# A tuned attention kernel: one of four head pairs goes from TensorE transposes to DMA transposes, with a new order

## The chip, the cores and the metric

The kernel runs on one core of a Trainium2 chip. The core has five engines with a queue each: TensorE (PE; its weight loads are shown as PEld), VectorE (DVE), ScalarE (ACT), GpSimd (POOL) and SyncE (SP), which here only issues transfers. The metric is the device time of one execution in microseconds (us); the median of three executions before the change is 809.87 us (809.32 to 811.25).

## The reference

Two attention layers follow each other. The first has 8 batches, 8 heads, 576 positions and 64 numbers a head. A score stays in the softmax only if it is within tau of its row's largest:

```python
scores = scale * np.matmul(q, k.transpose(0, 1, 3, 2))
thresh = np.max(scores, axis=-1, keepdims=True) - tau
scores = np.where(scores >= thresh, scores, -1000000000.0)
attn = softmax(scores)
x = concat_heads(attn @ v)              # 8 x 576 x 512
```

The second is a causal attention with four experts of one head each. Two of four experts are chosen for a position by gate logits, and their outputs are added with their weights:

```python
logits = x @ w_gate                     # the two largest of four, softmax over them: w
for e in range(4):
    a = softmax(causal(scale * (x @ wq[e]) @ (x @ wk[e]).T))
    out += w[..., e] * (a @ (x @ wv[e]) @ wo[e])
```

## The kernel before, in words

The 64 heads are worked on as 32 pairs, n = 0 to 31, four pairs a batch (n % 4 is 0 to 3). Both heads of a pair lie beside each other on the 128 partitions. The 576 queries of a head make four tiles of 128 and a rest of 64; the rests of two neighbouring pairs share one more tile, which comes with the odd pair. So an even pair has four query tiles and an odd pair five.

For each pair `prep` loads keys, queries and values (`ki`, `qi`, `vz`) and transposes keys and queries on PE into `kx` and `qx`. For each query tile, `scores` does this: PE multiplies (`kx`, `qx`) into PSUM, two banks a head (family "s"). DVE copies the scores to `pp` and takes the row's extreme (line 750). ACT applies the threshold (line 768) and the exponential with its sum (line 762). Then the paths part, by `on_pe(n)`:

- On PE: POOL scales `pp`. `transp` transposes it on PE in blocks (16 half transposes a tile, line 1306), DVE copies the blocks to `pa` (line 690), and ACT copies the rests to `pb`. `attnv32` multiplies with the values in fp32.
- By DMA: POOL writes the rounded half of `hl` in fp16 (line 716), and DVE the residual (line 739). `turned` issues one DMA transpose for the whole tile on SP's queue (`hl` to `T`, line 1032), and `attnv` multiplies in fp16, three products for one (the halves of weights and values). The values are split into fp16 halves `vh` once a pair, by a scale that comes from their largest number (a DVE reduction, a small PE product with `ones`, line 890, POOL, DVE line 739).

Before, the first four pairs (`FIRST = 4`) and of the later batches the third and fourth pair (`TURNED = 2, 3`) go on PE; the first and second pair of the seven later batches go by DMA: 7 x (4 + 5) = 63 transposes.

When a batch's four pairs are done, `moe` does the second layer for it: projections (fp32, rounded parts), gates, causal scores, transposes on PE, values and output. It is laid among the pairs of the next batch; only the last batch's has nothing beside it.

The order is not that of the code. Each operation is recorded with a place: a pair number plus a number from the table `PLACE`, and one by engine and tile from `PLACE_OP`. `arrange` goes through time with estimated durations, picks the ready operation of lowest rank for each engine, gives out buffers and PSUM banks, and so fixes the order of each engine's queue. Each engine then works its queue strictly in order. `fill` puts small matmuls on `still` into PE's planned gaps of the first 160 us. Buffers: two `hl`, three `T`, one `ki`, one `qi`, two `vz`.

Of the kernel before, what the change touches and what calls it, by code (L numbers as in the profile page):

```python
# [30 lines left out]
FIRST = 4  # L31
TURNED = 2, 3
# [50 lines left out]
    "ovload": -58.26292, "ovx": 0.6755247, "ovy": 0.919954, "perm": 3.2453, "qT": -0.3301571, "qload": 0.1930829,  # L83
# [102 lines left out]
class Plan:  # L186
# [43 lines left out]
    def op(self, e, busy, late, outs, ins, fn):  # L230
        o = Op(e, busy, late, outs, ins, fn, self.place)
        n = len(self.ops)
# [334 lines left out]
def kernel(  # L567
# [297 lines left out]
    def unit(n, name):  # L865
        plan.place = (n, ("", "o", "c", "d")[n % NPAIR] + name)
# [470 lines left out]
```

## Time and profile before

| | |
|---|---|
| median of 3 runs | 809.87 us |
| profiled execution | 809.53 us |
| its span, first to last instruction | 807.8 us |
| granted TensorE clock, mean | 0.997 |
| PE busy | 788.8 us (98%) |
| PE weight loads busy | 661.3 us (82%) |
| DVE busy | 678.7 us (84%) |
| ACT busy | 680.9 us (84%) |
| POOL busy | 346.3 us (43%) |
| DMA transposes T<-hl | 63, median 4.8 us from issue to landing |

An engine's busy time counts the instructions it carries out, not those that only issue a transfer. A group of instructions is shown with its busy time, the mean time of one, and the idle time of the engine just before it with what ended it. The chain of waits follows the last instruction back to the start, at each step to what released it.

### The profile page before, as it was taken

Reading aid. Unit: us, or ns where it says so; the run is one execution under the profiler, and the core shown is the slowest. Engines: PE = TensorE matmul, PEld = TensorE weight load, DVE = VectorE, ACT = ScalarE, POOL = GpSimd, SP = SyncE. Lnnn points to the kernel's source line nnn. Section 1 sums busy time; section 2 is a strip of 40 time slices with the busy share of each in tenths; the row PEclk is TensorE's granted clock in tenths of the full one; section 3 lists DMA queues with packets and bytes.
Section 4 is the critical chain, followed back from the end, with each engine's and each line's share of the span. In section 5 each row is a group of like instructions: output and inputs, shape, how many; then the busy total and the mean of one; then the engine's idle time right before and its main releaser. Section 6 shows DMA issues by size and latency. Waiting matters only on the chain.

```text
span 807.8 us, 27956 instructions
## 1 busy us (share of the span) xinstructions
PE 788.8 (98%) x10986; PEld 661.3 (82%) x10986; DVE 678.7 (84%) x2147; ACT 680.9 (84%) x1834; POOL 346.3 (43%) x494
## 2 busy tenths in 40 slices
PE   8999999999999999999999999999999999999998
PEld 6777888788778888788888897878878788878986
DVE  3889889988998889988899788998799888998284
ACT  3889889987999879898799988999799987989373
POOL 5764326433454326532275323643246432564110
PEclk9999999999999999999999999999999999999999
DMA  8431567427591356714575165642647227660002
GB/s 164 103 71 46 119 107 123 93 56 144 109 166 36 90 108 153 139 41 114 104 154 107 43 134 114 145 97 57 145 99 139 50 68 132 129 118 16 15 14 93
DMA packets 253604, 79.87 MB, mean 99 GB/s; under 512 B 240288, under 2 KB 248736, under 8 KB 253472
## 3 DMA queue, kind: packets, MB, share of 16 engines
q1 hardware_dynamic: 251744, 77.69, 46.7%
q8 instruction: 86, 1.41, 0.7%
q10 hardware_dynamic: 1728, 0.39, 0.3%
q14 instruction: 46, 0.38, 0.1%
HBM read 31.47 MB, written 9.44 MB: 51 GB/s over the span
## 4 chain that ended last, share of the span: by engine, by line
PE 69%; DVE 15%; DMA 6%; ACT 5%; issue 2%; POOL 1%; SPq 0%; POOLq 0%; ACTq 0%; DVEq 0%
PE banks L653 60%; PE banks L1306 9%; DVE pp L750 5%; DMA T<-hl 4%; DVE hl L739 2%; ACT pp L768 2%; DVE p L745 2%; DVE pa L690 2%; ACT pp L762 2%; DVE col L716 1%; DVE col L715 1%; POOL hl L716 1%; DMA lg<-in_moe_w_gate_dram 1%; DMA qi<-in_q_dram 0%; ACT pt L688 0%
## 5 line engine op out<-in xcount | busy, mean ns | idle before, releaser
L768 ACT ACTIVATE pp<-pp,col 128x576 f32<-128x576 f32 x286 | 212.1, 776 | 31.7 <-DVE col L716 27.1
L750 DVE TENSOR_SCALAR_CACHE_REDUCE pp<-banks 128x576 f32<-128x576 f32 x286 | 207.9, 749 | 16.4 <-PE banks L653 13.9
L762 ACT ACTIVATE pp<-pp 128x576 f32<-128x576 f32 x286 | 195.1, 685 | 1.0
L716 POOL TENSOR_SCALAR pp<-pp,col 128x576 f32<-128x576 f32 x160 | 123.9, 785 | 136.3 <-DVE col L728 88.9
L653 PE MATMUL banks<-kx,qx 64*128 64x288 f32 x1024 | 157.5, 422 | 0.8 <-DVE pp L750 0.3
L716 POOL TENSOR_SCALAR hl<-pp,col 128x576 f16<-128x576 f32 x126 | 93.7, 756 | 114.5 <-DMA T<-hl 37.7
L739 DVE SCALAR_TENSOR_TENSOR hl<-pp,col,hl 128x576 f16<-128x576 f32 x126 | 117.3, 944 | 29.5 <-POOL hl L716 29.5
L716 POOL TENSOR_SCALAR p<-p,col,gw 128x256 f32<-128x256 f32 (+3 forms) x114 | 75.9, 676 | 131.5 <-PE banks L653 49.8
L653 PEld LDWEIGHTS banks<-kx,qx 64*128 64x128 f32 x1024 | 92.2, 187 | 24.8 <-issue 4.7
L690 DVE COPY pa<-banks 128x512 f32<-128x512 f32 x152 | 96.8, 681 | 4.6 <-PE banks L1306 4.5
L762 ACT ACTIVATE p<-p,col 128x384 f32<-128x384 f32 (+4 forms) x136 | 78.4, 580 | 24.9 <-DVE col L745 24.0
L653 PE MATMUL banks<-pa,vz 128*64 128x128 f32 (+1 forms) x1344 | 82.0, 266 | 0.3 <-DVE pt L690 0.2
L745 DVE CUSTOM_DVE_ANT_0 p<-banks,mask 128x384 f32<-128x384 f32 (+4 forms) x136 | 66.1, 504 | 13.8 <-PE banks L653 13.8
L653 PEld LDWEIGHTS banks<-pa,vz 128*64 128x64 f32 x1344 | 68.8, 137 | 7.2 <-issue 3.0
L1306 PEld LDWEIGHTS banks<-ident,pp 64*128 64x128 f32 x1492 | 57.5, 139 | 15.6 <-issue 5.1
L653 PE MATMUL banks<-wvh,x 128*128 128x260 f32 x320 | 66.1, 289 | 2.9 <-DVE col L745 2.9
L1306 PE MATMUL banks<-ident,pp 64*128 64x64 f32 x1492 | 66.3, 227 | 1.3 <-DVE pp L750 0.7
L653 PEld LDWEIGHTS <-vh 128*64 128x64 f16 x2100 | 54.6, 111 | 11.2 <-DMA T<-hl 5.8
L653 PE MATMUL banks<-T,vh 128*64 128x128 f16 (+1 forms) x2100 | 59.0, 215 | 4.0 <-DMA T<-hl 3.3
L653 PEld LDWEIGHTS banks<-wvh,x 128*128 128x128 f32 x320 | 52.1, 188 | 8.7 <-DVE col L745 5.9
L688 ACT ACTIVATE pt<-banks 128x384 f32<-128x384 f32 (+2 forms) x128 | 56.9, 503 | 0.9 <-PE banks L1306 0.8
L762 ACT ACTIVATION_READ_ACCUMULATOR pp<-pp 128x1 f32 x286 | 57.5, 201 | 0.0
(143 smaller groups left out, 1623.6 us busy)
## 6 DMA issues: line engine op xcount, KB each, us to landing
ki<-in_k_dram SPq DMA_DIRECT2D x32, 256.0 KB, 3.7
vz<-in_v_dram SPq DMA_DIRECT2D x32, 256.0 KB, 2.8
qi<-in_q_dram SPq DMA_DIRECT2D x62, 128.0 KB, 2.9
out_dram<-st SPq DMA_DIRECT2D x30, 256.0 KB, 2.6
tk<-in_k_dram SPq DMA_DIRECT2D x16, 128.0 KB, 3.9
vz<-in_v_dram SPq DMA_DIRECT2D x64, 16.0 KB, 2.4
out_dram<-st SPq DMA_DIRECT2D x8, 128.0 KB, 2.3
T<-hl SPq DMA_TRANSPOSE x63, 4.8
```

The source lines that it names most:

```text
L653: lambda o, x, y: nc.tensor.matmul(o, x, y, start=start, stop=stop))
L688: run(e, t, [dst], [src], lambda d, s: nc.scalar.activation(d, s, AF.Copy))
L690: run(e, t, [dst], [src], lambda d, s: nc.vector.tensor_copy(d, s))
L715: return m.tensor_scalar(d, s, x_, None, op0=op0)
L716: return m.tensor_scalar(d, s, x_, y_, op0=op0, op1=op1)
L739: return nc.vector.scalar_tensor_tensor(d, a_, x_, r.pop(0), op0=op0, op1=op1, **kw)
L745: lambda o, a, i, m: nc.vector.tensor_tensor_reduce(o, i, m, 1.0, 3e38, ALU.add, ALU.min, a))
L750: lambda o, a, i: nc.vector.tensor_scalar(o, i, 1.0, None, op0=ALU.mult, op1=ALU.min, accum_out=a))
L762: return nc.scalar.activation(d, s, AF.Exp, scale=scale, **kw)
L768: lambda d, s, x: nc.scalar.activation(d, s, AF.Prelu, bias=x, scale=-1.0, alpha=1e36))
L1306: o.fn(*(r.place() for r in (*o.outs, *o.ins)))
```

## The change

- `TURNED = (3,)`: the third pair of the seven later batches goes by DMA transposes. 28 tiles change path: 7 x (4 + 5 + 4) = 91 transposes. `on_pe` also has a new term with `FINAL = 0`, which changes nothing at that value. The third pair's values are now split into `vh`.
- A head's two banks of scores may be any two of the eight, not only neighbours.
- For the first pair the keys come first on SP's queue and the queries first on ACT's, with the first two heads of the tails; tau and the first weights come after. The other heads' tails are loaded later, in their own transfers.
- All places of the order are new (`PLACE`, `PLACE_OP`; a new name for the place of `hl`, and the planned issue time of some transfers), of which a line or two is shown.

```diff
-TURNED = 2, 3
+TURNED = (3,)
+FINAL = 0
...
-    "LMo0": 37.77021, "LMo1": 59.55178, "LMo2": 59.18834, "LMo3": 6.447113, "LMo4": 4, "La00": 81.09086,
+    "LMo0": 83.62052, "LMo1": 44.69387, "LMo2": 32.21728, "LMo3": 16.53009, "LMo4": 4, "La00": 83.36004,
...
+PSUMS = "s", "g"
...
-    plan.family("s", [Slot([("b", i), ("b", i + 1)], lambda *_, i=i: banks[:, i:i + 2]) for i in range(7)])
+    plan.family("s", [Slot([("b", i), ("b", i + d)], lambda *_, i=i, d=d: banks[:, i:i + d + 1:d])
+                      for d in range(1, 8) for i in range(8 - d)])
...
-        busy = 580 if e == "SP" and more == 0 else 650
+        busy = 580 if e == "SP" and more == 0 else 700
...
-    plan.place = (-36.0, "load")
+    plan.place = (-320.0, "load")
     dma(tau_t, bass.AP(tensor=tau.tensor, offset=tau.offset, ap=[[0, P], [1, 1]]), "ACT", 1)
...
-        plan.place = (n, ("", "o", "c", "d")[n % NPAIR] + name)
+        plan.place = (n, ("", "o", "c", "d")[n % (2 if n >= NPR - FINAL else NPAIR)] + name)
 
     def on_pe(n):
-        return n < FIRST or n % NPAIR in TURNED
+        return n < FIRST or n % NPAIR in TURNED and n < NPR - FINAL
...
         if not n:
-            plan.place = (-30.0, "load")
+            plan.place = (-430.0, "load")
         dma(ki, ks, "SP", more)
         unit(n, "qload")
         if not n:
-            plan.place = (-29.0, "load")
+            plan.place = (-530.0, "load")
         for j in range(2):
             dma(qi[:, :, j], qs[:, :, j], eq, more)
         if n == 0 or n % NPAIR == 1 and b < B - 1:
-            plan.place = (n, "tload") if n else (-22.0, "load")
             c = b + (n > 0)
             tk, tq = (tails.setdefault((c, x), plan.tile(x, [P, H, D], F32)) for x in ("tk", "tq"))
-            for rows in heads:
-                dma(tk[rows], k[c, :, SM:, :].rearrange("h p d -> p h d"), "SP", more)
-            dma(tq[heads[0]], q[c, :, SM:, :].rearrange("h p d -> p h d"), eq, more)
+            for part in (slice(0, 2), slice(2, H)) if n == 0 else (slice(0, H),):
+                plan.place = (n, "tload") if n else (0.0, "tload0") if part.start else (-328.0, "load")
+                for rows in heads:
+                    dma(tk[rows, part], k[c, part, SM:, :].rearrange("h p d -> p h d"), "SP", more)
+                dma(tq[heads[0], part], q[c, part, SM:, :].rearrange("h p d -> p h d"), "SP" if part.start else eq, more)
...
-        unit(n, f"n{s}")
+        unit(n, f"h{s}")
         hl = plan.tile("hl", [P, 2, 2 * S], F16)
```

What the change moves is shown at three places. The first is PE in the middle of a later batch, at the first products of the third pair with its values. Before, the transposes of the pair's weights (`ident` with a `pp`) and the fp32 products (`pa`, `pb` with `vz`) stand there; `p`, `pt` and `q` are of the second layer:

```order
L653 MATMUL banks<-kx_66,qx_64 128x288 x4
L1306 MATMUL banks<-ident,pp_71 128x64 x16
L1306 MATMUL banks<-ident,p_76 128x64 x16
L653 MATMUL banks<-pa_111,vz_177 64x128 x8
L653 MATMUL banks<-pb_115,vz_177 64x128 x2
L653 MATMUL banks<-pa_113,vz_177 64x128 x8
L653 MATMUL banks<-pb_115,vz_177 64x128 x2
L653 MATMUL banks<-kx_66,qx_64 128x288 x4
```

Now, at the same products of a later batch, the fp16 products of `T` and `vh` stand there, 60 in all for two tiles, of which the first is shown:

```order
L660 MATMUL banks<-q_100,q_99 128x384 x2
L660 MATMUL banks<-kx_66,qx_64 128x288 x4
L1314 MATMUL banks<-ident,pp_67 128x64 x16
L660 MATMUL banks<-pt_110,v_98 64x64 x10
L660 MATMUL banks<-pt_108,v_98 64x128 x8
L660 LDWEIGHTS vh_74
L660 MATMUL banks<-T_83,vh_74 64x128
```

The transposes that still stand in the new rows (`pp_67`) are of the fourth pair; the third pair's are gone from PE.

The second place is DVE, at the third pair's tiles of a later batch. Before, it copies transposed blocks to `pa` between the evictions of scores (from `banks` to `pp`):

```order
L750 TENSOR_SCALAR pp_68,col_154<-banks 128x576
L690 COPY pa_112<-banks 128x8x64 x2
L750 TENSOR_SCALAR pp_68,col_154<-banks 128x576
L716 TENSOR_SCALAR col_152<-col_154,tau_p 128x2
L715 TENSOR_SCALAR col_143<-col_143 128x2
L728 RECIPROCAL col_143<-col_143 128x2
L699 TENSOR_TENSOR x_91<-banks,x_90 128x256
```

Now the residuals of the values (`vh`) and of the weights (`hl`) stand there:

```order
L757 TENSOR_SCALAR pp_69,col_122<-banks 128x576 x2
L746 SCALAR_TENSOR_TENSOR vh_74<-vz_177,col_149,vh_74 128x640
L723 TENSOR_SCALAR col_124<-col_122,tau_p 128x2
L706 TENSOR_TENSOR z_106<-banks,z_105 128x384
L746 SCALAR_TENSOR_TENSOR hl_79<-pp_71,col_141,hl_79 128x576
L722 TENSOR_SCALAR col_119<-col_119 128x2
L746 SCALAR_TENSOR_TENSOR hl_79<-pp_71,col_141,hl_79 128x576
```

Two copies from PSUM a tile have become two residuals from SBUF a tile, and the values' residual is one more.

The third place is the start of SP's queue. Before, the first weights (`st`, `lg`) and all tails of the first batch's keys (`tk`) stand ahead of the first pair's keys:

```order
L778 DMA st_72<-in_moe_wq_dram 128x4x64
L778 DMA st_73<-in_moe_wk_dram 128x4x64
L778 DMA lg_156<-in_moe_w_gate_dram 128x4
L778 DMA tk_84<-in_k_dram 64x8x64 x2
L778 DMA ki_61<-in_k_dram 128x8x64
L778 DMA vz_177<-in_v_dram 128x2x256
```

Now the keys are first, then the tails of two heads:

```order
L785 DMA ki_61<-in_k_dram 128x8x64
L785 DMA tk_84<-in_k_dram 64x2x64 x2
L785 DMA st_72<-in_moe_wq_dram 128x4x64
L785 DMA st_73<-in_moe_wk_dram 128x4x64
L785 DMA lg_156<-in_moe_w_gate_dram 128x4
L785 DMA tq_87<-in_q_dram 64x8x64
L785 DMA vz_177<-in_v_dram 128x2x256
```

Four issues have moved from ahead of the keys to behind them, but for two small tails that keep close to them.

## Rows read from the trace of the kernel before

**Rows 1.** The page: busy time by engine; the chain by engine.
```profile
PE 788.8 (98%) x10986; PEld 661.3 (82%) x10986; DVE 678.7 (84%) x2147; ACT 680.9 (84%) x1834; POOL 346.3 (43%) x494
...
PE 69%; DVE 15%; DMA 6%; ACT 5%; issue 2%; POOL 1%; SPq 0%; POOLq 0%; ACTq 0%; DVEq 0%
```

**Rows 2.** Windows: stretch, length, busy us of five engines, clock, DMA share, GB/s.
```profile
120.00:140.00 20.00, 19.85 (x351) 17.08 (x353) 19.35 (x54) 19.89 (x55) 13.85 (x19) 1.00 0.67 132
...
156.70:253.00 96.30, 94.72 (x1373) 79.78 (x1374) 85.05 (x272) 85.95 (x234) 41.89 (x56) 1.00 0.54 107
...
445.30:542.00 96.70, 94.77 (x1349) 79.63 (x1349) 84.85 (x269) 85.54 (x230) 41.87 (x56) 1.00 0.50 106
...
156.70:733.80 577.10, 567.96 (x8081) 477.26 (x8083) 506.98 (x1601) 510.09 (x1374) 251.22 (x336) 1.00 0.51 105
```

**Rows 3.** PE's timeline: start us, length, line, op, count, with idle time before.
```profile
450.33 1.09 PE L653 MATMUL banks<-pa,vz 128*64 128x128 f32 x16
...
452.67 1.40 PE L1306 MATMUL banks<-ident,pp 64*128 64x64 f32 x38
453.90 0.41 PE L1306 MATMUL banks<-ident,qi 64*128 64x64 f32 x8
...
494.41 1.87 PE L653 MATMUL banks<-T,vh 128*64 128x128 f16 x60
496.21 1.24 PE L653 MATMUL banks<-kx,qx 64*128 64x288 f32 x8
...
504.89 0.28 PE L653 MATMUL banks<-col,ones 128*64 128x1 f32 x4
505.03 1.85 PE L653 MATMUL banks<-T,vh 128*64 128x128 f16 x60
```

**Rows 4.** Groups by line and form: count | busy us, mean ns | idle before.
```profile
L739 DVE SCALAR_TENSOR_TENSOR hl<-pp,col,hl 128x576 f16<-128x576 f32 x126 | 117.3, 944 | 29.5 <-POOL hl L716 29.5
L690 DVE COPY pa<-banks 128x512 f32<-128x512 f32 x152 | 96.8, 681 | 4.6 <-PE banks L1306 4.5
...
L739 DVE SCALAR_TENSOR_TENSOR vh<-vz,col,vh 128x640 f16<-128x640 f32 x14 | 13.2, 946 | 0.0
...
L688 ACT ACTIVATE pb<-banks 128x128 f32<-128x128 f32 x54 | 11.8, 274 | 1.4 <-PE banks L1306 1.4
...
L724 DVE TENSOR_REDUCE col<-vz 128x1 f32<-128x640 f32 x14 | 11.3, 808 | 0.0
...
L890 DVE RECIPROCAL col<-col 128x1 f32<-128x1 f32 x14 | 2.2, 155 | 0.0
```

**Rows 5.** The tile hl: shortest/median/longest ns, first and last start; transposes to landing.
```profile
L739 DVE SCALAR_TENSOR_TENSOR hl<-pp,col,hl x126: 792/807/1344, 89.8 to 716.1; 128x576 f16<-128x576 f32 x126
...
DMA to landing us min/median/max: 4.6/4.8/6.7
```

**Rows 6.** Waits: engine and line, waited for, us in total, times, longest.
```profile
PEld L653 <- DMA T<-hl: 5.8, 5, 1.9
...
PE banks L653 <- DMA T<-hl: 3.3, 3, 1.2
...
SPq L778 <- PE banks L1306: 124.9, 41, 9.6
```

**Rows 7.** Timeline of the start: start us, length, queue or engine, idle before.
```profile
0.80 0.45 SPq L778 DMA_DIRECT2D st<-in_moe_wq_dram  x1
...
3.87 0.15 DVE L716 TENSOR_SCALAR tau_p<-tau_t 128x1 f32<-128x1 f32 x1 [2.78 <-DMA tau_t<-in_tau_dram]
...
4.53 0.63 SPq L778 DMA_DIRECT2D ki<-in_k_dram  x1
...
6.90 0.47 PE L1306 MATMUL banks<-ident,qi 64*128 64x64 f32 x8 [1.39 <-DMA qi<-in_q_dram]
...
10.39 0.37 PE L1306 MATMUL banks<-ident,ki 64*128 64x64 f32 x1
...
16.60 5.06 PE L1303 MATMUL banks<-still 128*128 128x256 bf16 x44
```

More of the change, by code (lines that the diff above doesn't have):

```diff
@@ L35 @@
     "F0": 0.2926676, "F1": 0.6107417, "F2": 0.7488845, "F3": 0.7924216, "Fv0": 0.7107417, "Fv1": 0.8924216,
[47 rows of a table removed]
-    "ovload": -58.26292, "ovx": 0.6755247, "ovy": 0.919954, "perm": 3.2453, "qT": -0.3301571, "qload": 0.1930829,
[4 rows of a table removed]
[29 rows of a table added]
+    "ctload": 21.58207, "ctt0": 0.7277149, "ctt1": 0.7604245, "cvload": 3.667135, "cvx": 0.7784061, "cvy": -0.8698999,
[8 rows of a table added]
+    "dtload": -2.15, "dtt0": 0.5876976, "dtt1": 1.164348, "dvload": 36.70649, "dvx": 0.6755247, "dvy": 0.919954,
[11 rows of a table added]
+    "ott0": 0.6700297, "ott1": 1.526483, "ovload": -27.53855, "ovx": 0.8599628, "ovy": -0.7607698, "perm": 3.2453,
[5 rows of a table added]
@@ L88 @@
 }
 PLACE_OP = {
-    "ACT gw": -110.6866, "ACT kx": 130.1295, "ACT lg": 28.07628, "ACT p2": -169.2215, "ACT pb": -76.67689,
-    "ACT pp": 62.41844, "ACT pt2": -63.89664, "ACT q2": 41.17327, "ACT q2d0": 1.945756, "ACT q2d1": -74.0949,
-    "ACT qi": 7.220311, "ACT qx": -6.128249, "ACT qz0": -104.6731, "ACT qz1": -30.00436, "ACT tau_t": 11.59095,
-    "ACT tq": 5.086954, "ACT v2": 68.15319, "ACT warm": 39.36742, "ACT wkh": 33.61568, "ACT woh": -31.10502,
-    "ACT wqh": -8.614884, "ACT wvh": -61.59402, "ACT x": 3.609935, "ACT z0": 22.39406, "ACT z1": 55.2578,
@@ L95 @@
-    "ACT zt": 100.1099, "DVE col": -76.00245, "DVE gate": -49.64892, "DVE gt": 55.0102, "DVE gw": -29.25879,
-    "DVE hl": 89.90104, "DVE kx": -3.083359, "DVE lg": 103.0635, "DVE p2": -56.31327, "DVE pa": -43.49546,
-    "DVE pp": -0.9060394, "DVE qsc": 13.38119, "DVE st": 48.42998, "DVE still": 16.89988, "DVE tau_p": -29.77201,
-    "DVE v2": -175.0338, "DVE vh": 29.35306, "DVE warm": -30.28686, "DVE x": 6.096136, "DVE z0": 86.35562,
-    "DVE z1": 35.242, "DVE zt": 32.66847, "POOL col": -52.95213, "POOL hl": 11.88103, "POOL ident": 35.86748,
@@ L100 @@
-    "POOL mask": 214.9782, "POOL mask2": -4.323271, "POOL ones": -59.24404, "POOL p2": -18.42273, "POOL pp": 1.127306,
-    "POOL q2d0": 39.59446, "POOL q2d1": -167.1478, "POOL qz0": 1.269118, "POOL qz1": -77.16671, "POOL st": -1.683233,
-    "POOL tie": -118.3152, "POOL vh": -15.23726, "POOL vz0": -30.97065, "POOL vz1": -4.521266, "POOL wkh": -7.741727,
-    "POOL wkl": -33.16535, "POOL woh": -1.366464, "POOL wol": 63.4879, "POOL wqh": 7.43681, "POOL wql": -5.369032,
-    "POOL wvh": -44.45069, "POOL wvl": -6.583584, "SP T": -127.4873, "SP ki": -31.62102, "SP lg": -38.43073,
@@ L105 @@
-    "SP out": -155.8852, "SP qi": 32.28295, "SP st": -120.1109, "SP tk": -42.89494, "SP tq": -50.62161,
-    "SP vz0": -89.02681, "SP vz1": 48.94072,
+    "ACT gw": -176.7795, "ACT kx": 109.051, "ACT lg": 32.86921, "ACT p2": -198.5523, "ACT pb": -66.55564,
+    "ACT pp": 102.2678, "ACT pt2": -46.66187, "ACT q2": 32.86169, "ACT q2d0": -18.15407, "ACT q2d1": -41.55532,
+    "ACT qi": 92.55249, "ACT qx": -56.52879, "ACT qz0": -120.712, "ACT qz1": -43.8384, "ACT tau_t": 5.010291,
+    "ACT tq": -13.62601, "ACT v2": 50.28766, "ACT warm": 61.07599, "ACT wkh": 33.61568, "ACT woh": -31.10502,
@@ new lines @@
+    "ACT wqh": -8.614884, "ACT wvh": -61.59402, "ACT x": 2.349036, "ACT z0": 76.6081, "ACT z1": 78.55429,
+    "ACT zt": 47.65369, "DVE col": -76.55561, "DVE gate": -77.11225, "DVE gt": 33.85956, "DVE gw": -44.70869,
+    "DVE hl": 143.9046, "DVE kx": -11.84931, "DVE lg": 91.45051, "DVE p2": -41.72111, "DVE pa": -19.85197,
+    "DVE pp": -24.61889, "DVE qsc": 79.4077, "DVE st": -5.024129, "DVE still": 60.11043, "DVE tau_p": -49.2988,
+    "DVE v2": -200.8968, "DVE vh": 26.28879, "DVE warm": -7.57284, "DVE x": 22.30481, "DVE z0": 53.22126,
@@ new lines @@
+    "DVE z1": 53.32278, "DVE zt": 63.44149, "POOL col": -52.95213, "POOL hl": 19.59957, "POOL ident": 48.47206,
+    "POOL mask": 193.4838, "POOL mask2": -31.25824, "POOL ones": -39.28948, "POOL p2": 1.28256, "POOL pp": 11.22654,
+    "POOL q2d0": 35.33228, "POOL q2d1": -221.3072, "POOL qz0": -17.73788, "POOL qz1": -72.36961, "POOL st": -38.80219,
+    "POOL tie": -108.033, "POOL vh": -8.494885, "POOL vz0": -10.81583, "POOL vz1": -62.98413, "POOL wkh": -10.41044,
+    "POOL wkl": -11.1327, "POOL woh": -51.74051, "POOL wol": 47.81164, "POOL wqh": 8.510708, "POOL wql": 26.90238,
@@ L107 @@
+    "POOL wvh": 7.740414, "POOL wvl": -7.853708, "SP T": -176.3157, "SP ki": -61.98671, "SP lg": -60.84482,
+    "SP out": -217.8366, "SP qi": 27.87735, "SP st": -109.4837, "SP tk": -34.68115, "SP tq": -116.2394,
+    "SP vz0": -67.61927, "SP vz1": 20.22504,
 }
@@ L245, in op @@
         for r in (*outs, *ins):
-            if r.v.fams[0] in ("s", "g"):
+            if r.v.fams[0] in PSUMS:
                 for b in self.banks(r):
@@ L257, in network @@
         ops, tiles = self.ops, self.virtuals
-        inside = lambda v: v.fams[0] in ("s", "g")
+        inside = lambda v: v.fams[0] in PSUMS
         of = list(range(len(ops)))
@@ L325, in arrange @@
         rank = {g: (ops[g].key + (PLACE_OP.get(ops[g].kind, 0.0) if ops[g].e != "PE" else 0.0), g) for g in members}
-        inside = lambda v: v.fams[0] in ("s", "g")
+        inside = lambda v: v.fams[0] in PSUMS
         turn = {}
@@ L369, in room @@
                         continue
-                    c = (k, 0.0 if f in ("s", "g") else ok, i)
+                    c = (k, 0.0 if f in PSUMS else ok, i)
                     if best is None or c < best[0]:
@@ L473, in loosen @@
         for v in self.virtuals:
-            if v.fams[0] in ("s", "g"):
+            if v.fams[0] in PSUMS:
                 v.span = (min(self.when[n] for n in v.ops), self.ends[v])
@@ L515, in fill @@
         for v in self.virtuals:
-            if v.fams[0] in ("s", "g"):
+            if v.fams[0] in PSUMS:
                 for _, b in v.slot.units:
@@ L671, in cost @@
         return 180 + (2.1 if slow else 0.95) * n
-    inps = lambda *xs: any(x.v.fams[0] in ("s", "g") for x in xs)
+    inps = lambda *xs: any(x.v.fams[0] in PSUMS for x in xs)
     def run(e, t, outs, ins, fn):
```

100 rows, old and new, of the table PLACE are left out of this document.

## The prediction, made before the changed kernel was run

> **What bounds the kernel now.** I read the page's busy shares and its chain of waits first, then the busy time by stretch, then PE's timeline inside one batch, the groups by line, and the waits. PE is busy 98% of the span, and 69% of the chain that ended last runs over PE, against 15% over DVE [rows 1]. From 156.7 to 733.8 us the same pattern comes six times, 577.1 / 6 = 96.2 us a batch [rows 2]. In such a batch PE is busy 94.7 us (idle 1.5), DVE 84.5 (88%), ACT 85.0 (88%), at the full granted clock (column 1.00), and the DMA engines half the time. So a batch is as long as PE's list of work, with two engines close behind. What the change takes from PE is gain until DVE or ACT becomes the limit; what it adds to DVE must fit into DVE's 11.7 idle us.
>
> **Part 1, the third pair by DMA.** Each of the seven batches after the first has one pair (n = 6, 10, ... 30) with four query tiles that changes its path.
>
> PE loses, per pair: the fp32 products with the values, two tiles from 450.33 to 452.67, 2.34 us, twice, 4.68; and the transposes, 38 of them from 452.67 to 453.90, 0.0324 us each, of which the pair has 4 x 16 + 8 = 72, 2.33 us. It gains the fp16 products, two tiles from 494.41 to 496.21, 1.80, twice, 3.60; and the small products that spread the maximum of the values, 504.89 to 505.03, 0.14 [rows 3]. Net 4.68 + 2.33 - 3.60 - 0.14 = 3.3 us a batch.
>
> DVE loses eight copies of transposed weights at 0.681 us (5.45) and gains eight residuals hl at 0.944 (7.55) and the value split: 0.946 + 0.808 + three small ones of about 0.155 (2.2) [rows 4]. Net 4.3 us more: 88.8 us a batch. ACT loses four copies of 0.274 us, 1.1 [rows 4], and stands at 83.9. POOL writes hl instead of pp, which is as much work.
>
> A residual takes 0.807 us in the median but up to 1.344 [rows 5]: it is stretched at times, and I have used the mean, which holds that. The Trainium skill (SBUF - State Buffer, "SBUF: two separate sides") says why that may be: a VectorE instruction with two SBUF inputs and a GpSimd instruction that reads SBUF share a port pair, and whichever is second blocks for the whole instruction. The old copies read PSUM and were free of that. By that rule the eight could all come out at the longest row, 8 x (1.344 - 0.944) = 3.2 us a batch more on DVE; the mean of 126 such instructions makes that unlikely, and it stays in the slower rival.
>
> How much of PE's 3.3 us is kept? If PE keeps its 1.5 us of idle time the batch is 91.4 + 1.5 = 92.9 us. If DVE cannot be filled better than now (88%), the batch is 88.8 / 0.878 = 101.1 us, longer than before. These are the two ends. The row nearest to the new load is the stretch 120 to 140 us: there PE, DVE and ACT are busy 19.85, 19.35 and 19.89 of 20 us at once, DVE 97% [rows 2]. So 95% is within reach of this program when the order is right, and an order laid out for the new mix should come close, though not over a whole batch, in which the projections give DVE little to do. I take 93.8 us: PE idle 2.4, DVE at 94.7%. That is 2.4 us a batch, x 7 = 16.8 us.
>
> Two waits are new for this pair. On DVE the residual waits for POOL's half of hl: 29.5 us in 126 so far [rows 4], 0.23 each, 1.9 us a batch for eight; the evictions of the next scores are queued behind it, and PE waits for those. That is less than half of the 5.0 us that DVE keeps idle in a batch of 93.8. On PE the fp16 products wait for T, with the transposes of the fourth pair and the second layer's scores queued behind them.
>
> The four more transposes a batch are issued on SP's queue, which waits most of the time (its longest wait group alone is 124.9 us), and land 4.8 us after issue (4.6 to 6.7) [rows 5, 6]. Were all of the DMA time of a batch (0.51 x 96.2 = 49 us) that of its nine transposes, four more would add 22 us: 71 of 93.8, still no limit. PE's waits for T so far are 5.8 + 3.3 us in the whole program [rows 6]. I take nothing for the new ones, as long as SP issues them in time; the end is in the rivals. A load queued behind a transpose on SP moves by the transpose's issue; as it is, the loads wait there for PE to free their buffers (the 124.9 us), so 0 until that slack is gone.
>
> **Part 2, any two banks.** The scores' evictions read as many elements as before: 0. What it frees is a wait for neighbouring banks, which shows in the trace only as part of PE's idle 1.5 us; it can give back no more than that, and I count it within the 93.8.
>
> **Part 3, the start.** Before, SP issues weights and tails first (0.80) and the first keys at 4.53; PE transposes them at 10.39, 5.9 us later; the queries are transposed at 6.90 [rows 7]. Now keys and queries are first on their queues. With the same 5.9 us the keys are there at 6.7, and PE has them after the queries, about 6.9 instead of 10.39: 3.5 us. Everything behind hangs on that chain: at 16.60 PE has only fillers ("still") until the first softmax comes back [rows 7]. The bounds are 0 (if the weights or the second pair, now later, hold up ACT and DVE) and 4.5 us (landing faster with nothing ahead). The tau load goes behind the queries; before it was there at 3.87, three us before it was needed [rows 7]; 0 to +1 us. The first tails are loaded in two halves, three more issues on a queue that mostly waits: 0. I take 3.5.
>
> **Part 4, the rest of the order.** In the tail the list on PE is nearly the same, with the same last rows; 0, within 3 us either way.
>
> **Sum.** Profiled execution 809.53 (span 807.8 and 1.7 around it): 809.5 - 16.8 - 3.5 = 789.2. It lies 0.3 below the median of the runs, so 789.5 us.
>
> **Rivals.** (A) is the forecast, 789.5; its own range is 783 to 798 (batch 92.9 to 95).
>
> (B) DVE becomes the bound, and it is slower. Place: the middle batches, where DVE has 88.8 us to do. Against: the stretch at 97% [rows 2]; for: in whole batches it never did better than 88%. It decides at a DVE share of 88.8 / 96.2 = 0.923: below that the batch is longer than now. At 0.90 the batch is 98.7, +2.5 x 7 = 17.5, less the start: 824 us. The Trainium skill (Perfetto Trace Analysis, "Identifying the Most-Contended Engine") speaks for this rival: matmul busy time is a poor measure and TensorE is to be judged by its weight loads. By that rule TensorE is at 477.26 / 577.1 = 83% [rows 2], ACT and DVE at 88% are the most contended, and work moved from PE to DVE goes the wrong way. Against it stands the chain, with PE at 69% [rows 1], and products that follow each other without a gap [rows 3].
>
> (C) Nothing is lost: PE keeps its idle 1.5, the batch is 92.9, 3.3 x 7 = 22.9; with the start 783 us, and 777 if the banks give back half of that idle time (0.75 x 7 = 5.3) and the start its 4.5. For: PE's idle time is small now with 98% asked of it. Against: DVE would have to work 96% of the time.
>
> (D) PE waits for transposes: of the 14 new groups of fp16 products each waits about as long as such a wait on PE lasted before (3.3 us in 3 times, 1.1; on the weight loads up to 1.9 [rows 6]); with 1.2 that is 16.8 us and the steady gain is gone: 806 us. For: the transposes share SP's queue with the loads, and hl has two buffers. Against: the order puts other pairs' work between.
>
> **Chances.** A 0.60, B 0.14, C 0.14, D 0.12. About 0.3% (2.4 us) is what a measurement of this kernel can tell from no change. A and C are faster; D ends just below the line, half of it faster; B is slower, a seventh of it within the line. Faster 0.60 + 0.14 + 0.07 = 0.81, same 0.05 + 0.02 = 0.07, slower 0.12. The range is 777 to 809: it takes in A, C and D and leaves out most of B and some 4 in 100 below.
>
> **What would show it.** The batch's period in the busy time by stretch: near 93.8, with PE over 97% and DVE at 94 to 95%. The first transposes of the keys near 7 us. T's waits on PE under 10 us in total. If the period is over 96 with DVE under 92%, and PE waits mostly for DVE's results, B is right; if PE waits for T by more than 15 us, D is. If PE's list of the third pair does not shrink by about 3.3 us, the first step is wrong.

## The result, and the profile after

The change made the kernel 0.6% slower: 815.69 us (median of 8, 812.72 to 818.42) against 811.04 (median of 8, 809.32 to 813.06) beside it, ratio 1.0056 [1.0033, 1.0079]. The forecast was 789.5. The profiled execution took 812.79 us with a span of 811.1, so it is one of the quicker ones; its span is 3.3 us above that of before. The times below account for these 3.3 us, not for the 4.65 between the medians. Page after, busy time by engine and the chain:

```profile
PE 774.7 (96%) x10815; PEld 642.9 (79%) x10815; DVE 687.2 (85%) x2182; ACT 679.4 (84%) x1806; POOL 355.4 (44%) x501
...
PE 61%; DVE 25%; DMA 5%; issue 4%; ACT 2%; POOL 2%; SPq 1%; POOLq 0%; DVEq 0%; ACTq 0%
```

Against [rows 1], PE lost 14 us of busy time, and DVE has 25% of the chain instead of 15%.

The scores are evicted by DVE 288 times in both kernels (line 750, now 757), 36 a batch. The start of the k-th, counted from 0, shows where the time went:

| eviction | before | after | difference |
|---|---|---|---|
| 0 | 13.6 | 9.5 | -4.2 |
| 12 | 33.4 | 33.4 | 0.0 |
| 24 | 58.1 | 51.8 | -6.3 |
| 48 | 111.6 | 115.1 | +3.5 |
| 84 | 203.8 | 210.0 | +6.2 |
| 264 | 685.8 | 687.3 | +1.5 |
| 287, the last | 740.3 | 747.3 | +7.0 |
| end of the span | 807.8 | 811.1 | +3.3 |

The start gains its 4.2 us. (Some 0.8 of them belong to the profiled execution of before: its granted clock was 0.50 from 7.8 to 11.2 us, and in runs below with the same start at full clock the first eviction comes at 12.7 to 12.9.) Then, up to eviction 84, 10.4 us are lost, 7.7 of them by eviction 48. (The -6.3 at eviction 24 is no gain: the new order has evicted earlier but transposed less by then.) The five batches from 84 to 264 gain 4.7 us, 0.94 each, where 2.4 each were forecast. Two runs below that differ from these two kernels only in their first issues take 95.75 and 96.47 us a batch there, so the gain is 0.7 to 0.9. The last batch loses 5.5 and the rest gives back 3.7. A part of that is work moved forward: PE is busy 56.5 us between evictions 264 and 287 against 53.9 before, and 59.5 behind them against 64.0.

The five batches in windows (columns as in [rows 2]), before and then after:

```profile
203.80:685.80 482.00, 473.47 (x6744) 397.83 (x6743) 422.76 (x1334) 425.26 (x1146) 209.35 (x280) 1.00 0.52 107
```

```profile
210.00:687.30 477.30, 462.87 (x6618) 385.53 (x6614) 427.86 (x1358) 423.39 (x1126) 214.27 (x285) 1.00 0.68 132
```

A batch went from 96.4 to 95.5 us. PE's busy time fell from 94.7 to 92.6, its idle time rose from 1.7 to 2.9. DVE rose by 1.0 us a batch, to 85.6 (89.6%), not by 4.3 to 94.7%.

PE's groups by form in the same stretches (count | busy us, mean ns | idle before), before:

```profile
L653 PE MATMUL banks<-pa,vz 128*64 128x128 f32 x640 | 42.5, 275 | 0.0
...
L653 PE MATMUL banks<-T,vh 128*64 128x128 f16 x1200 | 37.1, 220 | 3.3 <-DMA T<-hl 3.3
L1306 PE MATMUL banks<-ident,pp 64*128 64x64 f32 x810 | 35.3, 226 | 0.3
...
L653 PE MATMUL banks<-pb,vz 128*64 128x128 f32 x160 | 15.5, 273 | 0.0
```

and after:

```profile
L660 PE MATMUL banks<-T,vh 128*64 128x128 f16 x1816 | 56.5, 219 | 0.2 <-DMA T<-hl 0.2
...
L1314 PE MATMUL banks<-ident,pp 64*128 64x64 f32 x450 | 22.7, 227 | 0.3 <-POOL pp L723 0.3
L660 PE MATMUL banks<-pa,vz 128*64 128x128 f32 x320 | 21.1, 274 | 0.0
...
L660 PE MATMUL banks<-pb,vz 128*64 128x128 f32 x80 | 7.8, 273 | 0.0
```

T,vh gains 19.4 us, pa, pb and the transposes lose 21.4 + 7.7 + 12.6: net 22.3, 4.5 us a batch by these rows (they count overlapping records). So the third pair's work did go from PE, as forecast (3.3); PE's busy time shows 2.1 of it, the batch 0.94.

What PE and its weight loads wait for in these five batches after (us in total, times, longest):

```profile
PEld banks L660 <- DVE pp L757: 10.0, 18, 1.1
...
PE banks L660 <- DVE pp L757: 5.2, 10, 0.9
PE banks L1314 <- DVE pp L757: 4.0, 7, 1.0
...
PE banks L660 <- DMA T<-hl: 0.2, 1, 0.2
```

PE does not wait for T. It waits for DVE's evictions, which give the PSUM banks free; before, its longest were for T and for DVE's minima of the second layer (line 745):

```profile
PE banks L653 <- DMA T<-hl: 3.3, 3, 1.2
PE banks L653 <- DVE col L745: 2.9, 4, 1.4
```

The residuals and the POOL half that they follow, whole program after (to set beside [rows 4, 5]):

```profile
L723 POOL TENSOR_SCALAR hl<-pp,col 128x576 f16<-128x576 f32 x182 | 140.7, 786 | 169.0 <-DMA T<-hl 71.7
...
L746 DVE SCALAR_TENSOR_TENSOR hl<-pp,col,hl 128x576 f16<-128x576 f32 x182 | 159.4, 886 | 15.1 <-POOL hl L723 15.1
```

A residual takes 886 ns in the mean instead of 944, and DVE waits 15.1 us for POOL in 182 of them, less than before in 126 (29.5). POOL waits 71.7 us for a transpose to release a buffer.

### The profile page after: what moved, and what is told of

Its sections match the earlier page's. It is cut to its first block, busy times and chain, and to the rows that moved or that the text cites. A ratio compares the mean times of both kernels' runs of the same rounds, so it can differ in the third digit from the quotient of the medians.

```text
span 811.1 us, 27734 instructions
## 1 busy us (share of the span) xinstructions
PE 774.7 (96%) x10815; PEld 642.9 (79%) x10815; DVE 687.2 (85%) x2182; ACT 679.4 (84%) x1806; POOL 355.4 (44%) x501
## 4 chain that ended last, share of the span: by engine, by line
PE 61%; DVE 25%; DMA 5%; issue 4%; ACT 2%; POOL 2%; SPq 1%; POOLq 0%; DVEq 0%; ACTq 0%
PE banks L660 55%; DVE pp L757 8%; PE banks L1314 6%; DVE hl L746 4%; DMA T<-hl 4%; DVE p L752 3%; DVE col L723 2%; DVE pa L697 2%; DVE st L697 1%; DVE col L722 1%; DMA st<-in_moe_wq_dram 1%; ACT pp L775 1%; DVE col L735 1%; ACT pp L769 1%; SPq L785 1%
## 5 line engine op out<-in xcount | busy, mean ns | idle before, releaser
L757 DVE TENSOR_SCALAR_CACHE_REDUCE pp<-banks 128x576 f32<-128x576 f32 x284 | 206.5, 749 | 13.5 <-PE banks L660 11.2
L723 POOL TENSOR_SCALAR hl<-pp,col 128x576 f16<-128x576 f32 x182 | 140.7, 786 | 169.0 <-DMA T<-hl 71.7
L746 DVE SCALAR_TENSOR_TENSOR hl<-pp,col,hl 128x576 f16<-128x576 f32 x182 | 159.4, 886 | 15.1 <-POOL hl L723 15.1
L723 POOL TENSOR_SCALAR p<-p,col,gw 128x512 f32<-128x512 f32 (+3 forms) x116 | 76.8, 671 | 113.0 <-DVE col L735 59.8
L723 POOL TENSOR_SCALAR pp<-pp,col 128x576 f32<-128x576 f32 x102 | 80.0, 796 | 64.2 <-DVE col L735 35.1
L660 PE MATMUL banks<-T,vh 128*64 128x128 f16 (+1 forms) x2940 | 85.3, 216 | 0.9 <-DMA T<-hl 0.9
L697 DVE COPY pa<-banks 128x512 f32<-128x512 f32 x92 | 59.7, 677 | 0.2
L660 PE MATMUL banks<-x,wqh 128*128 128x288 f32 x256 | 53.9, 303 | 1.9 <-DVE col L723 1.0
L695 ACT ACTIVATE q<-banks 128x288 f32<-128x288 f32 x64 | 25.7, 401 | 35.1 <-PE banks L660 34.9
L660 PE MATMUL banks<-x,wkh 128*128 128x288 f32 x256 | 52.8, 298 | 0.0
L660 PE MATMUL banks<-pa,vz 128*64 128x128 f32 (+1 forms) x880 | 50.8, 258 | 2.1 <-DVE pp L757 2.1
```

What stands on the lines that cost most here:

```text
L660: lambda o, x, y: nc.tensor.matmul(o, x, y, start=start, stop=stop))
L695: run(e, t, [dst], [src], lambda d, s: nc.scalar.activation(d, s, AF.Copy))
L697: run(e, t, [dst], [src], lambda d, s: nc.vector.tensor_copy(d, s))
L723: return m.tensor_scalar(d, s, x_, y_, op0=op0, op1=op1)
L746: return nc.vector.scalar_tensor_tensor(d, a_, x_, r.pop(0), op0=op0, op1=op1, **kw)
L757: lambda o, a, i: nc.vector.tensor_scalar(o, i, 1.0, None, op0=ALU.mult, op1=ALU.min, accum_out=a))
```

## The experiments

My theory after the result (S in the texts below): DVE's queue paces PE in stretches of the new order, so PE's saving is lost there. Its rivals: PE's list still sets the batch and only start and end lost the gain (P), the waits behind the transposes and the two buffers of hl took it (B), or the new order did.

**Reliefs: one engine's work made shorter, the order kept.** If an engine's list sets the time, most of what is taken off comes back. The edits, the same in both kernels:

```diff
# less_pe: third fp16 product of pairs 0 and 1 left out
-matmul(gs[heads[j]], vh[:, x, f:f + D], ts[s][:, e][:, sub], c == 0 and k_ == 0, c == R and k_ == 2)
+matmul(gs[heads[j]], vh[:, x, f:f + D], ts[s][:, e][:, sub], c == 0 and k_ == 0, c == R and k_ == 2 - less)
+if less and k_ == 2:
+    plan.ops[-1].fn = lambda *_: None
# less_dve: stt(hl[:, 1, at], ...) on 432 of 576 columns, pairs 0 and 1, from the third batch on
+    d, a_, b_ = d[:, :cut], a_[:, :cut], b_[:, :cut]
# less_act: kinked on 432 of 576 columns, pairs 0 and 1, from the third batch on
+    nc.scalar.activation(d[:, :, :cut], s[:, :, :cut], AF.Prelu, ...
# less_pool: scaled(...) of pp and hl on 288 of 576 columns, all pairs, from the third batch on
# less_third: the residual of hl of the third pair on 64 of 576 columns, from the third batch on
```

> The changed kernel in its own order, with the third of the three fp16 products (T with the values' lower half) left out for the first and second pair: PE loses about 0.3 us a tile, 9 tiles a batch, 2.7 us a batch, 19 us in seven batches. Theory S (in the changed order DVE's queue paces PE in long stretches, so PE's savings are lost there): less than half comes back, 4 to 9 us, 807 to 812. Rival P (PE's list still sets the batch, and the change lost its gain only at the start and the end): 14 to 19 us, 797 to 802.

> The changed kernel in its own order, with the residual hl of the first and second pair cut from 576 to 432 columns from the third batch on (the rest of hl keeps old values): DVE loses about 0.15 us an instruction, 18 a batch, 2.7 us a batch, 16 us in six batches. Theory S: a third to a half comes back, 5 to 9 us, 807 to 811. Rival P: DVE is at 90% and has slack, under 2 us.

> The kernel before in its own order with the same products left out: PE loses the same 19 us. If PE's list sets the batch there, as I read it (98% busy), 13 to 19 us come back, 792 to 798; by theory S the old order gives back more than the new one. If the neighbours at 88% hold it already, under 9 us.

> The kernel before in its own order with the same residuals cut: DVE loses the same 16 us. Theory S: less than in the changed kernel, 0 to 4 us. If DVE's queue paces PE just as much in the old order, 5 us or more.

> The changed kernel in its own order, with the residual hl of the third pair (the work that the change adds to DVE) cut from 576 to 64 columns from the third batch on: DVE loses about 0.53 us eight times, 4.2 us in each of six batches, 25 us. Theory S, first form (DVE's queue sets the pace where the third pair's residuals stand, 718 to 748 us above all): 8 us or more comes back, 3 of them in the last batch. Theory S, second form (several engines are so close together that none alone gives much back, as the first relief runs read): 1 to 5 us.

> The changed kernel in its own order with three reliefs at once: the PE and DVE reliefs as before (2.7 us a batch each) and the threshold on ACT for the first and second pair cut from 576 to 432 columns from the third batch on (0.12 us, 18 a batch, 2.2 us a batch). PE alone gave 6.3 us by the medians, DVE alone 1.2. If none of the engines is the limit alone but all three are close, the reliefs together give more than their sum: 10 to 16 us, 800 to 806. If the limit lies elsewhere (waits behind transposes, buffers), the sum or less: 6 to 8 us.

> The kernel before in its own order with the same three reliefs. PE alone gave 3.8 us by the medians, DVE alone 2.6. Close together: 9 to 15 us, 795 to 801. Limit elsewhere: 4 to 7 us.

> The changed kernel in its own order with the relief of ACT alone (13 us in six batches). If ACT is the hidden limit that the reliefs of PE and DVE ran into: 6 us or more. Close together with the others: 1 to 4 us.

> The changed kernel in its own order, with POOL's scaling of pp and of the rounded half of hl cut from 576 to 288 columns from the third batch on (the rest keeps old values): POOL loses about 0.35 us an instruction, 36 a batch, 12 us a batch, of an engine that is busy 44%. If POOL has slack, as its share says: under 2 us. If the chain POOL, then DVE's residual, then the transpose paces stretches of the new order (POOL's half late, DVE held up behind it): 5 us or more.

> The kernel before in its own order with the same cut. If POOL has slack: under 2 us. If the chain paces the new order more than the old one: 1 to 4 us here, less than in the changed kernel.

> The kernel before in its own order with the threshold on ACT for the first and second pair cut from 576 to 432 columns from the third batch on, 13 us in six batches. PE, DVE and ACT relieved together gave 11.8 us, PE alone 3.8, DVE alone 2.6. If reliefs add up: 5 us here. If they help only together: 1 to 3 us.

All ratios are to the kernel before. What came back for the old order is (1 - ratio) x 811; for the new one it is counted from the changed kernel's 1.0056, whose own interval of +-0.0023 (1.9 us) comes on top.

| relief, us to be taken off | old order | came back | new order | came back |
|---|---|---|---|---|
| PE, 19 | 0.9956 [0.9943, 0.9968] | 3.6 | 0.9989 [0.9980, 0.9999] | 5.4 |
| DVE, 16 | 0.9967 [0.9955, 0.9979] | 2.7 | 1.0051 [1.0038, 1.0064] | 0.4 |
| ACT, 13 | 0.9974 [0.9964, 0.9983] | 2.1 | 1.0046 [1.0034, 1.0058] | 0.8 |
| PE, DVE, ACT, 48 | 0.9857 [0.9838, 0.9876] | 11.6 | 0.9964 [0.9952, 0.9976] | 7.5 |
| POOL, 76 (52 taken) | 0.9941 [0.9928, 0.9954] | 4.8 | 0.9994 [0.9982, 1.0006] | 5.0 |
| third pair's residual, 25 | | | 0.9985 [0.9974, 0.9995] | 5.8 |

By the groups' busy time the cuts took off, in the old and the new order, 17.4 and 18.1 us on PE, 16.2 and 15.1 on DVE, 12.9 and 12.9 on ACT, 52 and 51 on POOL, and 24.9 of the third pair's residuals. POOL's figure in the expectations was too high: an instruction lost 0.24 us.

The main finding is the first cell. In the old order, with PE busy 98%, 19 us off PE's list (17.4 by the group) gave 3.6 us. My expectation (13 to 19) was wrong. Theory S said that the old order would keep more of PE's saving than the new one; the new one keeps 28%, the old one 19%, two figures that their intervals don't tell apart (5.4 and 3.6 us, some 2 and 1 us of uncertainty). Theory S fails on the second row: 5 to 9 us were expected of DVE's relief in the new order, and 0.4 came, as rival P had it; P fails on the first row (14 to 19 expected, 5.4 came). The third pair's residual gave 5.8, short of the 8 of S's first form. No single engine gives back a third of its relief in either order. In the old order the three together give 11.6, more than their sum of 8.4 (some 1.6 us of uncertainty on either number); in the new order 7.5 against 6.6, which is no difference (10 to 16 were expected of engines close together). POOL, busy 43%, gives as much as PE when its instructions are made shorter: it stands in the chain from ACT's sum to the residual and the transposes. This cut was not POOL's alone, though: DVE's busy time fell with it by 11.4 us in the old order (678.7 to 667.3) and 7.7 in the new one, while its own instructions were left as they were; a residual took 897 ns instead of 944. At the rate of DVE's own relief in the old order (2.7 for 16) that is an estimated 2 of the 4.8 us. That it gives more in the new order (expected) is not borne out: 5.0 and 4.8.

Where PE's relief went can be read in the trace. before_less_pe, window of the five batches and PE's groups:

```profile
204.10:682.10 478.00, 468.28 (x6240) 389.90 (x6240) 422.08 (x1334) 425.12 (x1146) 209.23 (x280) 1.00 0.52 107
```

```profile
L653 PE MATMUL banks<-kx,qx 64*128 64x288 f32 x640 | 102.4, 423 | 0.0
...
L653 PE MATMUL banks<-T,vh 128*64 128x128 f16 x800 | 26.1, 220 | 3.5 <-DMA T<-hl 3.5
```

In the kernel before, the first of these groups reads:

```profile
L653 PE MATMUL banks<-kx,qx 64*128 64x288 f32 x640 | 98.1, 421 | 0.0
```

T,vh fell by 11.0 us, but PE's busy time only by 473.5 - 468.3 = 5.2. The same 640 products of kx,qx became 4.3 us busier with the same mean length: they overlap less, because they come further apart. One record lasts 0.42 us, while eight of them take 1.2 us (1.24 for x8 in [rows 3]); a wait of a tenth or two between two products is covered by the record of the first. PE's 98% held such waits, and PE's list had more slack than the 1.5 us of idle time.

**The change's loads in the old order.**

```diff
+# third pair, from n = 6 on: only products with c == 0, and pb of one head, are kept
+                    if less and c:
+                        plan.ops[-1].fn = lambda *_: None
+# third pair's copies to pa
+                nc.vector.tensor_copy(d, s)
+                if more:
+                    nc.vector.tensor_copy(d[:, :7], s[:, :7])
```

> The kernel before in its own order, with only the loads of the change put on its third pair: seven of ten fp32 products left out (PE 3.3 us less a batch), and each copy of transposed weights to pa followed by a second copy of 448 columns (DVE about 0.54 us more, eight times, 4.3 us a batch). No DMA transposes, no wait for POOL's half of hl, no new order. The forecast's step (PE less 3.3, 2.4 kept): 17 us gained, 794. Theory S (DVE's load alone takes it back): 0 to 6 us gained, 805 to 811. Slower than 811: DVE's load costs more than PE's saving gives.

840.31 us, ratio 1.0382 [1.0365, 1.0398]: 31 us slower. The window of the five batches:

```profile
209.65:713.99 504.34, 484.19 (x6464) 397.30 (x6463) 444.85 (x1374) 426.96 (x1146) 209.71 (x280) 0.97 0.50 102
```

A batch takes 100.9 us, 4.5 more, and DVE's busy time is 444.85 - 422.76 = 22.1 us more, 4.4 a batch. A part of this is TensorE's clock: it stood at its lower level (1.2 GHz, granted 0.50) for some 27 us of the window, in four of the five batches. The one batch at 1.00 throughout, in this run and then in the kernel before:

```profile
511.40:611.90 100.50, 96.86 (x1305) 79.25 (x1303) 89.46 (x278) 85.25 (x230) 41.91 (x56) 1.00 0.52 104
```

```profile
493.00:590.50 97.50, 94.83 (x1354) 79.72 (x1353) 84.98 (x268) 85.23 (x230) 41.87 (x56) 1.00 0.50 108
```

It is 3.0 us longer, with 4.5 us more on DVE. So most of the added DVE time is paid, and PE's saving isn't seen. That the place matters, since PE's products wait for just these copies, is argued: the waits of PE and its weight loads that are put down to `pa` rose only from 2.3 to 6.6 us in the five batches. The run doesn't say what 4.3 us cost elsewhere on DVE; it says that DVE's idle 11.7 us a batch did not take them in here.

**The start.**

```diff
+    for i, n in enumerate(first("SP ki", 1) + first("SP tk", 2) + first("ACT qi", 2) + first("ACT tq", 1)):
+        plan.when[n] = 700.0 + i          # before_keys_first; after_weights_first the other way round
```

> The kernel before in its own order, only the first issues moved: the first pair's keys, then its tails, first on SP's queue ahead of the first weights, queries first on ACT's ahead of tau. The forecast's step: 3.5 us gained at the first transposes and kept, 807.5. Rival: the gain is absorbed within the first 40 us, as in the changed kernel, 0 to 1 us.

> The changed kernel in its own order, only the first issues put back: two weights, the gate and the tails ahead of the first keys on SP's queue, tau ahead of the queries on ACT's. The forecast's step: 3.5 us slower. Rival (the gain is gone by 34 us anyway): within 1 us.

Keys first in the old order: 812.59, ratio 1.0033 [1.0021, 1.0045], 2.7 us slower, where the forecast's step and its rival both had a gain. Weights first in the new one: 818.48, ratio 1.0116 [1.0102, 1.0130], about 4.9 slower than the changed kernel; here the forecast's step (3.5 slower) comes near, and its rival (within 1) doesn't hold. Each order wants its own start. The chain of waits at the start of the kernel before shows why for the old one (start us, us, what):

```profile
7.51 3.64 DMA st<-in_moe_wv_dram
...
13.11 0.78 POOL wol L699
13.89 2.55 DMA st<-in_moe_wq_dram
...
16.52 0.41 POOL st L716
...
19.12 3.29 DMA qi<-in_q_dram
...
22.54 0.49 PE banks L1306 x9
```

and with the keys first:

```profile
15.40 2.61 DMA st<-in_moe_wq_dram
...
18.09 0.41 POOL st L716
...
21.06 3.58 DMA qi<-in_q_dram
...
24.78 0.49 PE banks L1309 x9
```

It doesn't run over the first keys. The weights go through two buffers `st`, which POOL empties; SP's queue waits for them, and the second pair's queries stand behind. Later weights make those queries 2.2 us later, and eviction 12 comes at 35.6 instead of 33.4, though the first comes 2.4 earlier (11.2 against 13.6). In the changed kernel the keys are transposed at 6.54 (10.39 before), and then PE has only fillers for 7.28 us (5.06 in [rows 7]):

```profile
6.54 0.22 PE L1314 MATMUL banks<-ident,ki 64*128 64x64 f32 x1
...
12.13 7.28 PE L1311 MATMUL banks<-still 128*128 128x256 bf16 x64
19.34 0.71 PE L1314 MATMUL banks<-ident,pp 64*128 64x64 f32 x16
```

With the weights first again, the new order's chain does run over the first keys. They are transposed at 7.94, only 1.4 us later, but the first eviction comes 3.1 later (12.6). PE had stood idle 1.14 us for the queries and 1.22 for the keys, and the granted clock was 0.50 from 7.6 to 14.4 us. The same products in the changed kernel and then in this run:

```profile
8.20 2.21 PE L660 MATMUL banks<-kx,qx 64*128 64x288 f32 x16 [0.19 <-ACT qx L693]
```

```profile
10.28 4.21 PE L660 MATMUL banks<-kx,qx 64*128 64x288 f32 x16
```

So of the 4.9 us a part, some 2 by these rows, is TensorE's clock.

**The buffers of hl, and the last batch.**

```diff
+    for i, v in enumerate(sorted((v for v in plan.virtuals if v.fams[0] == "hl"), ...)):
+        v.slot = slots[i % 3]             # after_hl3: three buffers instead of two
```

> The changed kernel in its own order with a third buffer for hl, given out in turn (its room is taken from the lower half of wo, whose product reads the upper half instead: same instructions, other values). It takes away POOL's waits for a buffer that a DMA transpose still reads (71.7 us in 32 waits). Rival B (the waits behind the transposes are what the change lost): 8 us or more gained. Theory S: DVE's own load is the limit in those stretches, 0 to 4 us.

> The changed kernel in its own order with the third hl buffer (wo's lower half replaced as before) and the third pair's residual cut to 64 columns from the fourth batch on. Each alone left the stretch from the 264th to the last eviction at 59.4 to 60.1 us (54.5 in the kernel before). If the transposes' waits and DVE's queue are two chains of the same length there: 55 to 57 us with both gone, and the total some 3 us below after_less_third. If it is the order itself: still 59 to 60.

A third buffer: 811.05, ratio 1.0021 [1.0011, 1.0031], 2.8 us better than the changed kernel's 1.0056, just outside each other's intervals, which come from different comparisons; rival B had 8 or more. POOL waited 71.7 us for a buffer of hl before (32 times); with three buffers no such wait is left, and in the profiled execution the evictions 48 to 287 come no earlier (0.2 us earlier to 1.9 later; the last at 747.6 against 747.3). It took 813.17 us, 2.1 more than that kernel's median, so the 2.8 us don't show in it. With the third pair's residual cut as well: 0.9992 [0.9979, 1.0004], no better than that cut alone (0.9985).

The last batch shows why such waits cost little. The chain of the changed kernel there:

```profile
718.66 1.44 DVE pp L757 x4
...
725.03 5.47 DMA T<-hl
...
730.81 6.22 DMA T<-hl
...
737.19 1.07 POOL hl L723 x2
...
741.54 0.78 ACT pp L775
...
747.31 0.78 DVE pp L757 x2
```

with three buffers (after_hl3):

```profile
719.10 1.44 DVE pp L757 x4
...
729.59 0.73 DVE hl L746
...
736.66 1.23 DVE hl L746
...
741.87 0.78 ACT pp L775
...
747.64 0.78 DVE pp L757 x2
```

and with the residual cut as well (after_hl3_third):

```profile
717.08 11.94 PE banks L660 x136
...
730.86 4.52 PE banks L660 x104
...
738.72 0.67 ACT pp L778
...
744.37 0.78 DVE pp L760 x2
```

First the transposes, then DVE, then PE: three chains of one length lie beside each other, and all end in ACT. From eviction 264 to 287 it takes 60.0, 60.1 and 59.6 us (59.4 with the cut alone), and 54.5 in the kernel before. My expectation of 55 to 57 was wrong. It is neither the transposes nor DVE's residuals, and no other relief moves it either: it takes 59.8 to 60.4 us in the changed kernel with less on PE, DVE, ACT, POOL or the first three at once. What is left is the order, with the banks that it gives out; that is argued, not shown.

**The first batch in the old order.**

```diff
+    order = plan.follow(SEQ, None)        # SEQ: places before 103 us as before, the rest as in the new order
```

> The changed kernel (third pair by DMA, any two banks, keys and queries of the first pair first on their queues), in which everything that stands before about 103 us in the old order is put in the old order, and the rest follows in the new one; buffers given out anew. If the new order of the first batch lost the 6 us: the 48th eviction of scores comes near 112 us as before, not at 115.1. If the start's loads or the banks lost it: still near 115. At the seam some us may be lost, so the total (805 to 816) tells less.

908.75 us, ratio 1.1216 [1.1198, 1.1235]. The 48th eviction comes at 130.8, and the kernel loses 8 to 19 us in each of the five batches (109.0 us in the mean, against 95.5), also where its order is the new one. The buffers and banks were given out by a simpler rule of mine, and that spoiled the test: it tells nothing of the first batch. It does show what they can cost. In the five batches DVE, ACT and POOL work the same instructions, by tile and form, in the same sequence as in the changed kernel, and PE's list differs in places. What grew most is PE's waits for the evictions that give banks free, in the changed kernel and then here (whole program):

```profile
PE banks L660 <- DVE pp L757: 11.7, 20, 1.1
```

```profile
PE banks L736 <- DVE pp L833: 66.2, 76, 1.4
```

In the kernel before the same wait took 0.3 us. So the banks are a rival to the order for what the change lost, and no run parts the two. The 10 us lost up to eviction 84 stay without a proven cause. 7.7 of them are gone by eviction 48, at 115.1 us, and the first values of a third pair are split at 146 us; up to there no pair's products have changed their path, which leaves the order, the first loads and the banks. That it is the order is argued, not shown.

**A version faster than both.** In `inverse`, the addition of 1e-9 to sums that are never below 1:

```diff
         scaled("DVE", x, x, EPS, op0=ALU.add)
+        plan.ops[-1].fn = lambda *_: None
         reciprocal(x)
```

> The kernel before in its own order, without the DVE instruction that adds 1e-9 to a sum of exponentials that is never below 1, ahead of the reciprocal (161 instructions of some 0.1 us of DVE's time, and one hand-over less in the chain from ACT's sum to POOL's scaling). If shortening that chain is kept as the relief of POOL was (4.8 us): 2 to 5 us gained, 806 to 809. If single reliefs of DVE are kept as before (a sixth): under 2 us.

805.85 us (805.59 to 807.59), ratio 0.9954 [0.9941, 0.9966], 3.7 us less than the kernel before: the fastest complete version here. DVE's busy time falls by 19 us (678.7 to 659.7), and a fifth of it comes back.

## Why the prediction was wrong

- **The bound.** "A batch is as long as PE's list of work" failed. I took PE's idle 1.5 us for its slack. The relief shows a list with more of it: 19 us off (17.4 by the group), 3.6 back.
- **What is kept.** I took 2.4 of 3.3 us a batch, 73%. Measured is 0.94 (28%), about what the reliefs of PE keep, 19% and 28%. This is the step that failed: 16.8 us were forecast from it, 4.7 came in five batches. The measured 95.5 us a batch lies between my two ends (92.9 and 101.1); the choice of 93.8 was wrong, which I had drawn from one stretch of 20 us in which three engines are full at once.
- **PE's list and DVE's load.** The third pair's work left PE as forecast. DVE's +4.3 was +1.0. By the groups the residuals of hl rose by 113.4 - 84.8 = 28.6 us in five batches and the copies fell by 57.1 - 32.3 = 24.8, and the mean residual took 882 ns instead of 945 in the same stretch. The values' residuals and maxima came to 4.4 and 4.1 more, so these four groups give 2.5 a batch; smaller groups and overlapping records make up the rest. That the residuals could all come out stretched, which I had drawn from the rule of the Trainium skill (SBUF - State Buffer, "SBUF: two separate sides"), did not come true; in the mean they were stretched less. The relief of POOL agrees with the rule itself: shorter POOL instructions took the mean residual from 944 to 897 ns in the old order.
- **Part 2, any two banks.** Not tried alone. PE's new waits are for banks that DVE's evictions give free, so they brought no relief that can be seen.
- **The start.** 3.5 us were forecast and 4.2 came at the first eviction (3.2 to 3.4 at equal clock; the 10.39 of [rows 7] lies in the stretch at 0.50), with the keys at 6.54 as said (near 7). By eviction 12 nothing is left of it. "Everything behind hangs on that chain" was wrong for the old order, where it hangs on the weights, two buffers and SP's queue. In the new order the early keys are needed (4.9 us without them) but bring no lead: the weights come next.
- **The rest of the order, 0 within 3.** What stands in this term lost 10.4 us up to eviction 84 and 5.5 in the last batch, less 3.7 at the end. This alone takes the steady gain and more. I put it at nothing because PE's list in the tail was nearly the same; the first batch wasn't in the reason. Whether the order or the banks lost it stays open.
- **The rivals.** D is refuted: PE waits 0.9 us for T in the whole program, and none of its weight loads' waits is put down to T. C is refuted too: nothing near 22.9 us was kept. B is half right: slower, and PE waits for DVE's evictions, but DVE is at 89.6%, its reliefs of 16 and 25 us give 0.4 and 5.8 back, and the period did not pass 96. The rule of the Trainium skill beside it (Perfetto Trace Analysis, "Identifying the Most-Contended Engine") was right that PE's matmul share misleads (98% busy, a fifth of the relief back). That DVE or ACT is the limit in its place does not follow: their reliefs keep no more than PE's.

## What to carry to other kernels

Before a gain is counted on an engine that is "98% busy", take some of its work away and measure what comes back; here a fifth did, in an order in which four engines hand each tile on. In these two orders a saving on one engine was mostly lost, presumably at the next hand-over, while work added in front of PE was mostly paid (3.0 of 4.5 us in the batch at full clock). A new order, with the banks that it gives out, is a change of its own, with its own error: here some 10 us against a gain of 5.

## What the runs showed of the hardware

A PE group's busy time can rise without more work (98.1 to 102.4 us, same 640 products, same mean), since records longer than the distance between two products cover short waits. With the same sequence on DVE, ACT and POOL, buffers and banks given out otherwise (and PE's list changed in places) took 109.0 us a batch against 95.5. With the granted clock at 0.50, after PE had stood idle 1.14 and 1.22 us, 16 products took 4.21 us instead of 2.21. And halving the columns of POOL's instructions made DVE's unchanged residuals shorter, 897 ns instead of 944.
